# Token weights loaded by SP's queue and cast on chip, state totals as a piece of their own, and a new written order, in a fused RWKV-7 and WaveMLP kernel

## The chip, the core and the metric

The kernel runs on one core of a Trainium2 chip. A core has five engines with instruction streams of their own: TensorE (PE), VectorE (DVE), ScalarE (ACT), GpSimd (POOL) and SyncE (SP). DMA engines, 16 for the core, move data for whichever engine issues a transfer. The metric is device time in microseconds (us); lower is better.

## The reference

The first part is a recurrence over 768 tokens for 4 batches and 8 heads, with a 40 x 40 state per head. The second part mixes channels and tokens of the result.

```
for t in range(S):                       # B,H,S,D = 4,8,768,40
    y[:, :, t] = einsum('bhd,bhde->bhe', r_t, state)
    Sa = einsum('bhde,bhe->bhd', state, a_t)
    state = state * w_t[:, :, None, :] - einsum('bhd,bhe->bhde', Sa, b_t) \
          + einsum('bhd,bhe->bhde', v_t, k_t)
x = y.transpose(0, 2, 1, 3).reshape(B, S, H * D)      # 4 x 768 x 320
theta = x @ w_theta
zr, zi = x * cos(theta), x * sin(theta)
y2 = einsum('ts,bsd->btd', w_tok_r, zr) + einsum('ts,bsd->btd', w_tok_i, zi)
u = x + y2
out = u + maximum(u @ w_ch, 0)
```

The inputs and the output are float32.

## The kernel before

The tokens are cut into 24 chunks of 128 tokens (6 per batch); each chunk has its tokens on the 128 partitions and all 8 heads of 40 channels beside one another. Within a chunk the recurrence is turned into matrix products; from chunk to chunk of a batch only a small state (`gt`) goes on. Decay is made for two chunks at once: the logarithm of w (`LN`, ACT), sums of it along the tokens on PE (`CSI` inclusive, `CSE` exclusive, with the totals that the state needs), and their exponentials on ACT (`INVW`, `WI`). Then k and b are multiplied by the inverse decay (`KH`), a by the decay (`AH`), all are transposed on PE (`TRK`, `TRA`, `TRR`, `TRV`), and four score products of 128 x 128 per head are made (`PSI`, `PHI`, `LV`, `LU`), masked while they are taken out of PSUM (on DVE), or copied on ACT and masked on POOL (`MPSI` and the like). `X0`, `NU`, `GT` and `Y` use them. A chunk's result x goes through a transpose (`XT`), the product with w_theta (`TH`), cosine and sine on ACT (`SIN`), and a product with x (`ZR`). When a batch has its z, the token mixing follows (`YR`, 12 products for each of 6 blocks of rows), then u (`EU`), its transpose (`UT`), the channel product (`CH`), the output (`EO`) and its store (`ST`).

An entry of the order that starts with E is the eviction of a result from PSUM: `EXT` after `XT`, `EWT` after `WT`, `ENX` and `ENU` (negated copies) after `X0` and `NU`, and so on. A letter after an entry names its engine (A ACT, V DVE, G POOL). S stands for a DMA transpose through the crossbar, issued by SP in place of transposes on PE with an eviction. `@n` names a PSUM bank.

The order of the work is written out as the string `ORDER`. A loop at the end of the kernel runs through it and records each entry's instructions; every engine then runs its own in that order, so that an instruction that waits holds back all that stand behind it on its engine. `GI` adds the old state on PE, `EGA` does the same on DVE; a chunk has one or the other.

The token weights `w_tok_r` and `w_tok_i` (768 x 768, float32 in memory) come in rows of 128 x 768: `LDT:tb.n` is load number tb of weight n. Before, POOL issues it as a DMA that casts to bfloat16, into one of three buffers for each weight (`row_load`, line 723). `WT` transposes the row by six PE transposes, `EWT` copies it into place. Nearly all other loads are issued by SP, in the order's sequence; of the first ones, four (`LDK:0A`, `LDA:0A`, `LDB:1A`, `LDV:0A`) are issued by ACT. The landing buffers of k, b, a and v hold five chunks each, those of r and w three pairs. A load into a buffer in use waits on the issuing engine for its last reader.

Score products and decay sums use 64 of the array's 128 rows at a time, in two halves; all other matmuls use 128.

Of the kernel before, what the change touches and what calls it, by code (L numbers as in the profile page):

```python
# [19 lines left out]
LDW:0 LDK:0A LDB:0 LDA:0A LDA:1 LDB:1A LDK:1 LDV:0A LN:0A LDC:0.0G LDT:0.0G CSI:0@0 LDC:0.1G CSE:0@1 WI:0A  # L20
INVW:0A KH:0V TRK:0@0 AH:0V EKBT:0A TRA:0@3 LDW:2 EAT:0V LDR:0 KH:1V PHI:0@1 PSI:0@0
EPSI:0A MPSI:0G CV:0A LDB:2 EPHI:0A AH:1V TRK:1@1 EKBT:1V LN:2A TRA:1@2 MPHI:0G LDV:1 TRV:0@3
LDK:2 X0:0@0 EAT:1V CSI:2@0 CR:0A ENX:0V LDA:2 PSI:1@1 INVW:2A EVT:0V NU:0 ENU:0A EPSI:1V
TRR:0@1 PHI:1@0 LDB:3 ERT:0A GT:0@2 CV:1A LDK:3 CSE:2@1 EPHI:1V TRV:1@3 ERT:1A NUT:0@0 KH:2G
WI:2A EGT:0V LV:0@0 LDA:3 EVT:1V X0:1@1 ENX:1A ENUT:0A ELV:0V LDV:2 AH:2G GD:0@2 LDR:2 TRK:2@3
KH:3G LV:1@1 NU:1 EKBT:2A LU:0@0 ELV:1V LDW:4 TRA:2@0 ENU:1A LDV:3 ELU:0A NUT:1@3 AH:3G EAT:2V
GT:1@1 ENUT:1V PSI:2@1 TRK:3@0 EGD:0V EPSI:2V LDK:4 LDA:4 GI:1 EKBT:3A CV:2G TRA:3@3 LU:1@0
ELU:1A CR:2G PHI:2@1 EGT:1V X0:2@2 EAT:3V EPHI:2V MLU:0G ENX:2A LN:4A LDB:4 TRR:2@0 PSI:3@0
LDR:4 CV:3G PHI:3@1 MLU:1G Y:0@1 EPSI:3A MPSI:3G EPHI:3V NU:2 TRV:2@3 CSE:4@0 LDV:4 ENU:2A
ERT:2A EVT:2V GT:2@2 EX:0V WI:4A AH:4G CSI:4@1 INVW:4A Y:1@3 LDW:6 NUT:2@1 EGA:2V EGT:2V ERT:3A  # L30
ENUT:2V LV:2@0 LDA:5 TRV:3@2 EX:1V X0:3@1 ELV:2A KH:4G EVT:3V LU:2@1 ENX:3V ELU:2V LV:3@0
TRA:4@0 ELV:3A LDK:5 NU:3 TRK:4@3 LDB:5 GD:1@2 EAT:4V ENU:3A MLV:2G XT:0@0 EKBT:4V CR:4A GT:3@1
GI:3 EGD:1V EGT:3V PSI:4@1 EPSI:4V CV:4G PHI:4@0 LN:6A TRR:4@3 EPHI:4A NUT:3@2 MLV:3G Y:2@1
ENUT:3V LDB:6 LDA:6 AH:5G LDK:6 CSI:6@1 X0:4@2 EX:2V EXT:0A ERT:4A INVW:6A TRV:4@0 ENX:4V
MPHI:4G LDV:5 KH:5G LU:3@0 ERT:5A XT:1@1 NU:4 ELU:3V EXT:1A CSE:6@1 LDV:6 LDT:1.1G ENU:4A
TRA:5@3 WI:6A NUT:4@1 EVT:4V ENUT:4A TRK:5@2 LDK:7 EAT:5V AH:6G XT:2@0 EKBT:5V LV:4@0 TH:0@3
ELV:4V KH:6G PSI:5@1 GD:2@1 LDR:6 SIN:0A TH:1@2 LU:4@0 CV:5G GT:4@3 GI:4 EXT:2A EPSI:5V CV:6G
ZR:0G LDW:8 TRA:6@0 PHI:5@1 LDB:7 ELU:4A LDA:7 EGD:2V EGT:4V TH:2@1 SIN:1A EAT:6V MLU:4G SIN:2A
TRK:6@3 X0:5@0 GD:3@2 EPHI:5V EKBT:6V ENX:5A LDB:8 Y:3@1 ZR:1G EGD:3V EX:3V PSI:6@0 EPSI:6V
TRV:5@3 TRV:6@2 Y:4@1 LN:8A LDK:8 NU:5 PHI:6@1 EVT:6V ENU:5V EVT:5A CR:6G X0:6@2 EPHI:6V  # L40
LDT:1.0G KH:7G TRR:6@0 ENX:6A CSI:8@0 INVW:8A LDA:8 LDV:7 EX:4V NUT:5@3 LV:5@1 ELV:5A LDB:9
ERT:6V AH:7G ENUT:5V TRK:7@1 CSE:8@0 ERT:7V KH:8G TRA:7@3 WI:8A LDV:8 LV:6@1 EAT:7V EKBT:7V
ELV:6A LU:5@0 LDA:9 GD:4@0 NU:6 ELU:5V AH:8G PSI:7@1 TRK:8@3 LDK:9 ENU:6A EGD:4A CV:7A MLV:5G
PHI:7@0 EKBT:8A ZR:2G GT:6@1 NUT:6@2 EPSI:7V EPHI:7A EGT:6V TRV:7@0 TRA:8@3 ENUT:6V LDW:10
X0:7@1 EVT:7V LU:6@1 ENX:7V LV:7@0 LDR:8 ELU:6V Y:5@2 EX:5V EAT:8A XT:3@0 MPHI:7G AH:9G NU:7
EXT:3V XT:4@3 ELV:7A PSI:8@1 EXT:4A GD:6@2 KH:9G EPSI:8A EGD:6V TRA:9@0 LDV:9 PHI:8@0 TH:3@3
# [90 lines left out]
def kernel(  # L137
# [124 lines left out]

    tiles = [T() for _ in range(N)]
    keep = tc.keep_in_program_order
    queue = {"": nc.sync, "A": nc.scalar}
    eng = {"A": nc.scalar, "V": nc.vector, "G": nc.gpsimd}

    def copy(e, out, in_):
# [383 lines left out]
    def ev_three(i, e, name, src, tag, held):  # L652
        if e == "S":
            crossbar(i, name, xp, tag, held)
            return
# [178 lines left out]
```

## Time and profile before

| | us |
|---|---|
| median of 3 runs (206.68 to 207.59) | 207.25 |
| the profiled execution | 206.92 |
| its span, from the first to the last instruction | 205.2 |
| PE busy | 190.1 |
| DVE busy | 170.6 |
| ACT busy | 154.3 |
| POOL busy | 147.1 |

The granted TensorE clock was 0.999 of full speed. In the profile's rows, `L278` and `L282` are the helpers that record every matmul and every transpose, `L270`, `L272` and `L275` those for copies and products, so groups are told apart by tiles: `sc` and `sm` are the PSUM tiles of scores and of the rest, `kb`, `ah`, `v`, `r` the scaled inputs, `kbT`, `aT`, `rvT` their transposes. A row of groups reads: line, engine, operation, output <- inputs, shapes, count, then busy us and mean ns of one, then the engine's idle time ahead of them and what ended it. A row of the stretches of time gives, for each engine, busy us and the number of instructions. A row of the timeline gives start, length, and what it is. `ACTq` and `SPq` are issues of DMAs by those engines. "DMA to landing" counts from the issue.

### The profile page before, as it was taken

What the parts mean: (1) busy time and instruction counts of PE and PEld (TensorE: products, weight loads), DVE (VectorE), ACT (ScalarE), POOL (GpSimd) and SP (SyncE); (2) the same over time, 40 slices, a digit from 0 to 9 for tenths busy, and PEclk for the clock granted to TensorE, in tenths of its full rate; (3) what the DMA queues carried; (4) which work ended last, traced back from release to release, by engine and by line L of the source; (5) the groups of instructions that cost most, each with busy time, mean ns of one, the idle gap of its engine ahead of it and who ended that gap; (6) DMA issues with size and microseconds to landing.
All of it is one profiled execution on the core that took longest, in us unless ns stands there. A gap on an engine that the chain in (4) does not pass through costs nothing.

```text
span 205.2 us, 7809 instructions
## 1 busy us (share of the span) xinstructions
PE 190.1 (93%) x3266; PEld 147.5 (72%) x3266; DVE 170.6 (83%) x334; ACT 154.3 (75%) x259; POOL 147.1 (72%) x157
## 2 busy tenths in 40 slices
PE   0389999999999999999999999999999999999992
PEld 0166777877777887887887877887877787777671
DVE  7256899999999997999799998989888797975653
ACT  2367799997989997999899788987898685822100
POOL 8225778899989699998966886993989785634000
PEclk9999999999999999999999999999999999999999
DMA  7999999998898999899489989987979996433342
GB/s 136 187 240 159 225 171 178 173 230 140 153 221 154 213 159 216 164 213 226 103 171 193 192 172 238 192 135 161 169 97 154 218 129 140 99 90 103 102 150 96
DMA packets 144802, 34.17 MB, mean 167 GB/s; under 512 B 139520, under 2 KB 144768, under 8 KB 144768
## 3 DMA queue, kind: packets, MB, share of 16 engines
q1 hardware_dynamic: 138176, 30.26, 76.5%
q0 software_dynamic: 2432, 2.77, 8.4%
q10 hardware_dynamic: 4160, 0.66, 2.2%
q8 instruction: 25, 0.41, 0.9%
q14 instruction: 9, 0.07, 0.1%
HBM read 29.13 MB, written 3.93 MB: 161 GB/s over the span
## 4 chain that ended last, share of the span: by engine, by line
PE 80%; ACT 6%; DVE 5%; issue 2%; ACTq 2%; POOL 2%; POOLq 0%; DVEq 0%
PE sm L278 39%; PE sc L278 22%; PE sm L282 20%; ACTq L331 1%; ACT kbT L270 1%; ACT psi L270 1%; DVE phi L275 1%; ACTq L326 1%; ACT Wi_two L412 1%; ACT lw_two L338 1%; POOL z L275 1%; DVE lamu L275 1%; DVE rvT L272 1%; POOL lamv L554 1%; POOL phi L554 1%
## 5 line engine op out<-in xcount | busy, mean ns | idle before, releaser
L275 POOL TENSOR_TENSOR kb<-raw_kb,invW_two 128x640 bf16<-128x640 f32 x22 | 33.9, 1542 | 5.5 <-ACT invW_two L373 3.6
L275 POOL TENSOR_TENSOR z<-cs,x 128x640 bf16<-128x640 f32 x22 | 30.8, 1403 | 5.3 <-ACT cs L677 5.3
L278 PE MATMUL sm<-z,wtok_r 128*128 128x320 bf16 x120 | 34.3, 299 | 0.0
L278 PE MATMUL sm<-z,wtok_i 128*128 128x320 bf16 x120 | 34.2, 299 | 0.0
L275 POOL TENSOR_TENSOR ah<-raw_a,Wi_two 128x320 bf16<-128x320 f32 x22 | 19.0, 866 | 8.5 <-issue 5.2
L275 DVE TENSOR_TENSOR psi<-sc,mask_p 128x1024 bf16<-128x1024 f32 x16 | 19.5, 1219 | 1.0 <-PE sc L278 0.9
L554 POOL TENSOR_SCALAR_AFFINE_SELECT psi<-psi 128x1024 bf16<-128x1024 bf16 x8 | 8.7, 1093 | 14.0 <-ACT psi L270 11.6
L275 DVE TENSOR_TENSOR phi<-sc,mask_p 128x1024 bf16<-128x1024 f32 x14 | 17.1, 1219 | 1.6 <-PE sc L278 1.4
L278 PE MATMUL sc<-aT,kbT 64*128 64x128 bf16 x384 | 17.3, 225 | 1.1 <-ACT kbT L270 0.7
L275 DVE TENSOR_TENSOR lamu<-sc,mask_p 128x1024 bf16<-128x1024 f32 x14 | 17.1, 1220 | 0.6 <-PE sc L278 0.3
L282 PE MATMUL sm<-ident,kb 128*128 128x128 bf16 x184 | 14.9, 227 | 2.6 <-DVE kb L275 2.3
L278 PEld LDWEIGHTS <-wtok_r 128*128 128x128 bf16 x144 | 14.0, 97 | 4.6 <-issue 0.3
L270 ACT COPY rvT<-sm 128x512 bf16<-128x512 bf16 x28 | 15.9, 593 | 1.3 <-PE sm L282 0.7
L278 PEld LDWEIGHTS <-wtok_i 128*128 128x128 bf16 x144 | 14.1, 98 | 3.9 <-issue 0.2
L275 DVE TENSOR_TENSOR lamv<-sc,mask_p 128x1024 bf16<-128x1024 f32 x13 | 15.9, 1220 | 1.0 <-PE sc L278 0.5
L677 ACT ACTIVATE cs<-sm 128x320 f32<-128x320 f32 x26 | 9.9, 452 | 8.5 <-PE sm L278 8.4
L278 PEld LDWEIGHTS <-kbT 64*128 64x128 bf16 x384 | 11.9, 97 | 5.8 <-issue 2.4
L278 PEld LDWEIGHTS <-rvT 64*128 64x128 bf16 (+1 forms) x272 | 13.6, 95 | 2.9 <-issue 0.5
L278 PE MATMUL sm<-kb,lamv 128*128 128x40 bf16 x192 | 15.0, 180 | 0.0
L278 PE MATMUL sm<-kb,lamu 128*128 128x40 bf16 x192 | 14.9, 179 | 0.0
L282 PEld LDWEIGHTS <-kb 128*128 128x128 bf16 x184 | 11.5, 101 | 4.2 <-DVE kb L275 2.3
L554 POOL TENSOR_SCALAR_AFFINE_SELECT lamu<-lamu 128x1024 bf16<-128x1024 bf16 x10 | 10.9, 1090 | 4.1 <-ACT lamu L270 4.1
(137 smaller groups left out, 625.0 us busy)
## 6 DMA issues: line engine op xcount, KB each, us to landing
raw_w_two<-in_w_dram SPq DMA_DIRECT2D x12, 320.0 KB, 4.8
raw_r_two<-in_r_dram SPq DMA_DIRECT2D x12, 320.0 KB, 4.8
out_dram<-oo SPq DMA_DIRECT2D x24, 160.0 KB, 2.5
raw_kb<-in_b_dram SPq DMA_DIRECT2D x23, 160.0 KB, 4.6
raw_a<-in_a_dram SPq DMA_DIRECT2D x23, 160.0 KB, 4.5
raw_kb<-in_k_dram SPq DMA_DIRECT2D x23, 160.0 KB, 4.3
raw_v<-in_v_dram SPq DMA_DIRECT2D x23, 160.0 KB, 4.7
wtok_row<-in_moe_w_tok_r_dram POOLq DMA_DIRECT2D x6, 192.0 KB, 4.8
```

The source lines that it names most:

```text
L270: keep(nc.scalar.copy(out=out, in_=in_))
L272: keep(eng[e].tensor_copy(out=out, in_=in_))
L275: keep(eng[e].tensor_tensor(out=out, in0=in0, in1=in1, op=ALU.mult))
L278: keep(nc.tensor.matmul(out, lhsT=lhsT, rhs=rhs, start=start, stop=stop, skip_group_check=True))
L282: keep(nc.tensor.transpose(out=out, in_=in_, identity=ident))
L326: keep(queue[e].dma_start(out=tiles[i].raw_kb[:, j], in_=source(ap, i)))
L331: keep(queue[e].dma_start(out=t, in_=source(ap, i)))
L338: keep(nc.scalar.activation(out=q.lw[:, :, :, 0:D], in_=q.raw_w.rearrange("p h (j d) -> p j h d", j=2), func=AF.Ln))
L412: keep(nc.scalar.activation(out=two, in_=q.cse[:, LO:LO + 2 * DM + 16], func=AF.Exp))
L554: keep(nc.gpsimd.affine_select(out=flat, in_=flat, compare_op=ALU.is_ge, fill=0.0, base=-1, pattern=[[0, 2 * G], [1, 128]], channel_multip ...
L677: keep(nc.scalar.activation(out=cs[i % 5][:, c], in_=tiles[i].theta, func=AF.Sin, bias=(math.pi / 2, 0.0)[c]))
```

## The change

Three things are changed, and the order is written anew.

The rows of the token weights are loaded by SP as float32 into one landing buffer for each weight (`wraw`), and cast by a new entry `CW` on ACT (5 times) or POOL (7 times) into one bfloat16 buffer for each weight (`wrow`, three before). `WT` then works as before.

The totals of the decay over a chunk, nine small matmuls, are taken out of `CSE` and become the entry `CST`, which may stand anywhere between `CSE` and `WI`.

No load is issued by ACT any more. There are three theta buffers in place of four. The functions also get a way to handle two chunks' last 64 channels in one product (`THR`, `CHR`, `twin_x`, `twin_u`, `mix_ends`); the order holds no such entry, so the sets are empty and `XT`, `TH`, `UT` and `CH` do what they did.

In the new order the kinds of entries change as follows: `GI` from 5 to 8 and `EGA` from 11 to 8; `UT` from 14 to 19 and `XT` from 19 to 17, `GD` from 15 to 16, `NUT` from 20 to 21, `TRV` from 22 to 23, and so crossbar transfers from 28 to 22; PE runs 3290 matmuls and transposes in place of 3266. `ENX` and `ENU` on ACT go from 24 to 37, on DVE from 24 to 11; `ERT` and `EVT` on ACT from 28 to 19, on DVE from 18 to 28; masked evictions of scores on DVE from 57 to 59, on ACT from 39 to 37. ACT's table loads go from 14 to 12. The first row of the token weights is loaded behind the loads of chunk 9, not at the start.

```diff
@@ ORDER: the start, and the last rows of the token weights
-LDW:0 LDK:0A LDB:0 LDA:0A LDA:1 LDB:1A LDK:1 LDV:0A LN:0A LDC:0.0G LDT:0.0G CSI:0@0 LDC:0.1G CSE:0@1 WI:0A
-INVW:0A KH:0V TRK:0@0 AH:0V EKBT:0A TRA:0@3 LDW:2 EAT:0V LDR:0 KH:1V PHI:0@1 PSI:0@0
...
+LDC:0.2G LDW:2 LDW:0 LDB:0 LDK:0 LDC:0.0G LDA:0 LN:2A CSE:2@0 LDK:1 LDB:1 LN:0A CST:2 CSI:0@1
+WI:2A INVW:0A CSE:0@0 CST:0 WI:0A KH:0V LDV:0 LDA:1 TRK:0@0 AH:0V TRA:0@3 CSI:2@1 EAT:0V KH:1V
...
-    wrow = ctx.enter_context(tc.tile_pool(name="wrow", bufs=3))
+    wraw = ctx.enter_context(tc.tile_pool(name="wraw", bufs=1))
+    wrow = ctx.enter_context(tc.tile_pool(name="wrow", bufs=1))
...
-    th = mw.tile([128, 4, DM], FP32, name="th")
+    th = mw.tile([128, 3, DM], FP32, name="th")
...
@@ def cse(i, b):
             pair_sums(q.cse, q.lw, pair_exc)
-            tot = q.cse[:, LO + 2 * DM:LO + 2 * DM + 16]
-            mm(tot, ident, off_two.rearrange("p a g c -> p (a g c)"), True, False)
-            for g in range(G):
-                for j in range(2):
-                    mm(tot.rearrange("p (a n) -> p a n", a=2)[:, :, 2 * g:2 * g + 2],
-                       q.lw[:, j, 2 * g:2 * g + 2, :].rearrange("p a b -> p (a b)"),
-                       halves, False, j == 1)
             return
...
+    def totals(i):
+        q = tiles[i]
+        tot = q.cse[:, LO + 2 * DM:LO + 2 * DM + 16]
+        mm(tot, ident, off_two.rearrange("p a g c -> p (a g c)"), True, False)
+        for g in range(G):
+            for j in range(2):
+                mm(tot.rearrange("p (a n) -> p a n", a=2)[:, :, 2 * g:2 * g + 2],
+                   q.lw[:, j, 2 * g:2 * g + 2, :].rearrange("p a b -> p (a b)"),
+                   halves, False, j == 1)
...
     def row_load(tb, n):
-        wrows[tb, n] = tile_of(wrow, [128, S], BF16, f"wtok_row_{n}")
-        keep(nc.gpsimd.dma_start(out=wrows[tb, n],
-                                 in_=moe_w_tok[n][tb * 128:(tb + 1) * 128, :]))
+        wrows[tb, n] = tile_of(wraw, [128, S], FP32, f"wtok_raw_{n}")
+        keep(nc.sync.dma_start(out=wrows[tb, n], in_=moe_w_tok[n][tb * 128:(tb + 1) * 128, :]))
+
+    def row_cast(tb, n, e):
+        t = tile_of(wrow, [128, S], BF16, f"wtok_row_{n}")
+        copy(e, t, wrows[tb, n])
+        wrows[tb, n] = t
...
+        "CSE": lambda i, j, e, b: cse(i, b), "CST": lambda i, j, e, b: totals(i),
+        "LDT": lambda i, j, e, b: row_load(i, j), "CW": lambda i, j, e, b: row_cast(i, j, e),
```

How the instructions stand on three engines is shown next, each before and after. In the names a number is that of a buffer. First ACT, from its start: `raw_w_two` is the loaded w of a pair of chunks, `lw_two` its logarithm, `Wi_two` and `invW_two` the decay and its inverse. Before:

```order
L798 ACT_TABLE_LOAD
L326 DMA raw_kb<-in_k_dram 128x8x40
L331 DMA raw_a<-in_a_dram 128x8x40
L326 DMA raw_kb<-in_b_dram 128x8x40
L331 DMA raw_v<-in_v_dram 128x8x40
L338 ACTIVATE lw_two_93<-raw_w_two 128x16x40
L412 ACTIVATE Wi_two<-sc_237 128x656
L373 ACTIVATE invW_two<-sc_231 128x640
```

And ACT's start after (`lw_two_94` is the pair of chunks 2 and 3):

```order
L846 ACT_TABLE_LOAD
L357 ACTIVATE lw_two_94<-raw_w_two 128x16x40
L357 ACTIVATE lw_two_93<-raw_w_two 128x16x40
L434 ACTIVATE Wi_two<-sc_222 128x656
L392 ACTIVATE invW_two<-sc_240 128x640
L434 ACTIVATE Wi_two<-sc_249 128x656
L289 COPY kbT<-sm_270 128x1024
```

The four loads are gone from ACT, and the logarithm and decay of the second pair stand ahead of the inverse decay and the decay of the first.

Second PE, at the decay sums of chunks 20 and 21 (`pair_exc` is the triangle of ones that makes the sums, `off_two` and `halves` belong to the totals). Before:

```order
L278 LDWEIGHTS pair_exc
L278 MATMUL sc_3883<-lw_two_93,pair_exc 128x320
L278 LDWEIGHTS ident
L278 MATMUL sc_3883<-off_two,ident 128x16
L278 LDWEIGHTS lw_two_93
L278 MATMUL sc_3883<-halves,lw_two_93 128x2x2
```

And PE there after (`rvT` holds r and v transposed, so this is a score product, `LV` of chunk 18):

```order
L297 LDWEIGHTS pair_exc
L297 MATMUL sc_3884<-lw_two_93,pair_exc 128x320
L297 LDWEIGHTS rvT
L297 MATMUL sc_3889<-rvT 128x128
L297 LDWEIGHTS rvT
```

The totals, which use all 128 rows, no longer follow the sums; a score product, which uses 64 like the sums, does.

Third SP, in the stretch in which the loads of chunks 10 to 12 stand. Before (`x2` is two such loads in a row):

```order
L331 DMA raw_a<-in_a_dram 128x8x40
L326 DMA raw_kb<-in_k_dram 128x8x40
L326 DMA raw_kb<-in_b_dram 128x8x40 x2
L326 DMA raw_kb<-in_k_dram 128x8x40
L320 DMA raw_w_two<-in_w_dram 128x8x80
L331 DMA raw_v<-in_v_dram 128x8x40
```

And SP there after:

```order
L760 DMA wtok_raw_1676<-in_moe_w_tok_r_dram 128x768
L345 DMA raw_kb<-in_k_dram 128x8x40
L325 DMA raw_r_two<-in_r_dram 128x8x80
L760 DMA wtok_raw_1755<-in_moe_w_tok_i_dram 128x768
L350 DMA raw_v<-in_v_dram 128x8x40
L345 DMA raw_kb<-in_k_dram 128x8x40
L345 DMA raw_kb<-in_b_dram 128x8x40
L760 DMA wtok_raw_1892<-in_moe_w_tok_r_dram 128x768
L760 DMA wtok_raw_1922<-in_moe_w_tok_i_dram 128x768
L339 DMA raw_w_two<-in_w_dram 128x8x80
```

Four row loads of the token weights now stand among the chunk loads; each of these four goes into the buffer of an earlier row and waits for that row's cast, and the loads behind it wait with it.

333 lines of the change are left out of this document (184 added, 149 removed).

## Prediction

> **What bounds the kernel now.** I read the page's busy times, then its row of slices and the chain that ended last, then the busy time of four stretches.
>
> ```profile
> PE 190.1 (93%) x3266; PEld 147.5 (72%) x3266; DVE 170.6 (83%) x334; ACT 154.3 (75%) x259; POOL 147.1 (72%) x157
> PE   0389999999999999999999999999999999999992
> PE 80%; ACT 6%; DVE 5%; issue 2%; ACTq 2%; POOL 2%; POOLq 0%; DVEq 0%
> ```
>
> The last chain of work lies on PE for 80% of the span, and PE's slices are full from the fourth on. The stretches (PE, PE's weight loads, DVE, ACT, POOL; then clock, DMA share, GB/s) tell where it isn't full:
>
> ```profile
> 0.00:20.00 20.00, 10.29 (x117) 7.59 (x117) 10.87 (x56) 10.36 (x15) 9.24 (x20) 1.00 1.13 184
> 20.00:70.00 50.00, 48.50 (x995) 37.90 (x992) 47.28 (x79) 45.14 (x77) 42.94 (x45) 1.00 0.98 182
> 70.00:200.00 130.00, 129.74 (x2153) 101.39 (x2149) 110.48 (x197) 98.47 (x170) 94.92 (x93) 1.00 0.83 161
> 200.00:205.20 5.20, 1.58 (x11) 0.59 (x9) 1.92 (x5) 0.38 (x1) 0.00 (x0) 0.98 0.27 95
> ```
>
> There are three regimes. Up to 20 us PE idles for 9.7 us, and the DMA engines are full (share 1.13). From 20 to 70 us PE, DVE (47.28 of 50) and ACT are close together. From 70 to 200 us PE is busy for 129.74 of 130 us, so there a new order can win only by giving PE less to do. How PE's time is made up shows one row by row (start, length, instruction):
>
> ```profile
> 126.44 0.30 PE L278 MATMUL sm<-z,wtok_i 128*128 128x320 bf16 x1
> 126.57 0.33 PE L282 MATMUL sm<-ident,x 128*128 128x128 bf16 x3
> 126.74 0.30 PE L278 MATMUL sm<-z,wtok_r 128*128 128x320 bf16 x1
> 126.88 0.30 PE L278 MATMUL sm<-z,wtok_i 128*128 128x320 bf16 x1
> 127.11 0.62 PE L278 MATMUL sc<-aT,kbT 64*128 64x128 bf16 x16
> 127.66 0.31 PE L278 MATMUL sm<-z,wtok_r 128*128 128x320 bf16 x1
> ```
>
> Read the starts. A 320-column matmul takes 0.135 us until the next one starts (126.44 to 126.57), three 128-column transposes 0.17 (0.055 each). But ahead of the score matmuls, which use 64 rows of the array (64*128), the same 320-column matmul takes 0.23 (126.88 to 127.11). The step from 128 rows to 64 costs 0.095 us more, with nothing waited for. I take the same for the step back, which the row of 16 merges.
>
> **The change part by part.** The profiled execution took 206.92 us, with a span of 205.2; the median of the runs shown is 207.25, 0.33 above it.
>
> *PE's own work.* In the lists of matmuls the 64-row blocks (scores and decay sums, 120 in both) stand next to one another at 36 places before, at 53 after; splitting off the state totals lets a decay sum join a score block. Each joint saves a step in and a step out: 17 x 2 x 0.095 = 3.2 us. Against it stand 24 more matmuls (fewer transposes go by the crossbar, and three more old states are added on PE): 21 x 0.055 + 3 x 0.135 = 1.6 us. Net -1.6, on the path wherever PE is the limit. Ends: nothing, if all of it falls where DVE holds PE, and -3.2 if the added matmuls fill idle time. I take -1.6, since 130 us of the span are of the third regime.
>
> *The head.* ACT's rows, the landing of the first w load (counted from its issue), the first product on DVE, and two pieces of the chain:
>
> ```profile
> 0.83 0.49 ACTq L326 DMA_DIRECT2D raw_kb<-in_k_dram  x1
> 2.09 1.54 ACTq L326 DMA_DIRECT2D raw_kb<-in_b_dram  x1
> 3.65 1.71 ACTq L331 DMA_DIRECT2D raw_v<-in_v_dram  x1
> 5.41 0.74 ACT L338 ACTIVATE lw_two<-raw_w_two 128x640 bf16<-128x640 f32 x1 [3.33 <-DMA raw_w_two<-in_w_dram]
> 7.83 0.72 ACT L412 ACTIVATE Wi_two<-sc 128x656 f32<-128x656 f32 x1 [1.68 <-PE sc L278]
> 8.44 0.70 ACT L373 ACTIVATE invW_two<-sc 128x640 f32<-128x640 f32 x1
> ...
> DMA to landing us min/median/max: 4.0/4.0/4.0
> ...
> 9.17 0.83 DVE L275 TENSOR_TENSOR kb<-raw_kb,invW_two 128x640 bf16<-128x640 f32 x1 [3.76 <-ACT invW_two L373]
> ...
> 15.56 0.64 ACT lw_two L338
> 16.24 1.15 PE sc L278 x12
> ```
>
> w landed at 0.81 + 4.0 = 4.8 us, but ACT was issuing loads until 3.65 + 1.71 = 5.36, and the first logarithm starts at 5.41. Afterwards ACT issues nothing, two w loads go first, and three things change. (a) ACT is free when w lands; but w of chunk 0 is now second on SP, so it lands between 4.8 us and, with 320 KB more ahead of it at 184 GB/s, 1.8 later at 6.6. (b) The inverse decay comes ahead of the decay of its own pair, which took 0.72. From the start of the logarithm to the first kb product passed 9.17 - 5.41 = 3.76 us; 3.04 are left of it, so that the product starts between 7.9 and 9.6, a move of -1.3 to +0.5. (c) The second logarithm and its sums, on the chain at 15.56 and 16.24 (1.8 us), are done early, and the first row of the token weights, 1.2 us of all DMA engines, leaves the stretch where those are full. I take -1.5: the middle of that move, -0.4, and -1.1 of the 3.0 in (c), since the loads that follow still share full DMA engines. Ends: +0.5, and -3 (-1.3 and over half of (c)).
>
> A rule weighed there: the Trainium skill, "DMA: Bandwidth & Descriptors", section "Issuing engines are not separate DMA queues", says that DMAs of all issuing engines run on the same 16 DMA engines and a second issuer saves sequencer time only. By that rule taking four loads from ACT's queue delays no landing and the head gains up to 3; by the row, where ACT's first issue overlaps SP's, it could lose 0.5. The share of 1.13 with both queues at work agrees with the rule.
>
> *Row loads and casts.*
>
> ```profile
> L723 POOL DMA_DIRECT2D wtok_row<-in_moe_w_tok_r_dram x6 | 3.5, 580 | 0.0
> L272 POOL CAST r<-raw_r_two 128x640 bf16<-128x640 f32 x7 | 5.0, 720 | 0.0
> L270 ACT CAST r<-raw_r_two 128x640 bf16<-128x640 f32 x5 | 3.6, 729 | 0.0
> L677 ACT ACT_TABLE_LOAD x7 | 9.0, 1283 | 0.1
> L521 ACT ACTIVATE nx<-sm 128x320 bf16<-128x320 f32 x11 | 4.9, 442 | 2.1 <-PE sm L278 2.1
> L270 ACT COPY rvT<-sm 128x512 bf16<-128x512 bf16 x28 | 15.9, 593 | 1.3 <-PE sm L282 0.7 <-DVE rvT L272 0.5
> L523 DVE TENSOR_SCALAR nx<-sm 128x320 bf16<-128x320 f32 x13 | 6.4, 489 | 2.3 <-PE sm L278 2.0
> L272 DVE COPY rvT<-sm 128x512 bf16<-128x512 bf16 x18 | 8.8, 491 | 0.8 <-PE sm L282 0.7
> L275 DVE TENSOR_TENSOR psi<-sc,mask_p 128x1024 bf16<-128x1024 f32 x16 | 19.5, 1219 | 1.0 <-PE sc L278 0.9
> ...
> DMA to landing us min/median/max: 4.0/4.8/6.3
> ...
> raw_w_two<-in_w_dram SPq DMA_DIRECT2D x12, 320.0 KB, 4.8
> ```
>
> POOL loses twelve issues (12 x 0.58 = 7.0 us) and gains seven casts of 768 columns, 0.72 x 768/640 = 0.86 each, 6.0: nothing either way, with POOL busy 72%. ACT gains five casts, 5 x 0.87 = 4.4, and 13 negated copies at 0.44 (5.7), and loses nine copies of r and v at 0.59 (5.3) and two table loads at 1.28 (2.6); with its smaller moves about +2. DVE gets ten such copies (4.9) and two masked products (2.4) and loses 13 negated copies (6.4): about +0.5. ACT's +2 spreads over 185 us in which it is busy three quarters, so PE's work covers it; uncovered, it would cost 2.
>
> What has a price is SP's queue, which takes over 16 loads (twelve rows, four from ACT) and loses six of 28 crossbar transfers; the bytes are the same, so the DMA engines' work is too. A row's landing buffer is single, so from its third row load on SP stops until the cast of an earlier row is done, and the loads of k, b, a, v, r, w wait behind it. The places are close: behind the sixth row load stands w of pair 12, whose logarithm comes 129 matmuls after the cast that is waited for; 130 us / 2153 = 0.060 us per matmul makes that 7.8 us. From it go the cast (0.87), the row load's share of all DMA engines (1.2) and the landing (4.8): 0.9 us is left. Between the two casts of rows 3 and 4 on POOL stand 107 matmuls, 6.4 us, against a cast and a landing of 5.7. A landing at the slow end (6.3) turns both into waits of about 0.7. Bounds: 0, and +6 (ten such loads at 0.6). I take +1.0, near the lower end, because 4.8 is the usual landing.
>
> *Everything else that the new order moves* (where evictions stand, three theta buffers in place of four, the end): +0.2. The nearest row is PE's 0.26 us of idle time in 130 us, which a new order can hardly better and can easily miss: between 0 and +3, taken near the lower end, as the last 5 us stand almost as they did.
>
> Sum: -1.6 - 1.5 + 1.0 + 0.2 = -1.9, so 205.0 for the profiled execution and 205.3 for the median.
>
> **The rivals.** *DVE holds the middle.* With 47.28 of 50 us busy from 20 to 70 us and 0.5 more to do, DVE gives back the head's lead and the joints there: -1.6 x 130/200 = -1.0 stays, +1.0 for the loads: 206.9, median 207.2, no change. For it: the DVE row. Against it: its work starts earlier too.
>
> *The loads come late (slower).* Place: SP's queue behind the row loads. Point: a row landing over 5.6 us after its issue. Eight of the ten stops then cost PE the 0.7 worked out above, 5.6 in place of 1.0: 209.6, median 209.9. For it: the largest landing, 6.3, and a DMA share of 0.98. Against it: loads have little to answer for in the list of waits (total, times, longest):
>
> ```profile
> POOL psi L554 <- DMA raw_kb<-in_k_dram: 2.5, 1, 2.5
> POOL kb L275 <- DMA raw_kb<-in_b_dram: 1.7, 1, 1.7
> ```
>
> *The casts cost ACT.* ACT's five casts stand ahead of evictions for which PE waits: 4.4 us are uncovered, 205.0 + 4.4 = 209.4, median 209.7. Against it: ACT's 75%. In the Trainium skill, "DMA: Bandwidth & Descriptors", section "Rules for kernel authors" has a cast during DMA issued from GpSimd, which is what the change gives up; no run so far shows which is cheaper here.
>
> *The late crossbar transfers were no loss.* PE's list of waits names none of them, so counting them brings nothing by itself; no term of the sum rests on it.
>
> **How the numbers follow.** Forecast 0.52; DVE holds 0.17; late loads 0.18; casts 0.05; a new wait elsewhere in the order 0.08, slower. Half a per cent, about what a measurement of this kernel can tell from no change, is 1.0 us: 206.2 to 208.3. Faster takes the forecast and a little of the second (0.56), the same most of the second (0.17), slower the rest (0.27). The range goes from 202.7 (head -3, loads 0, joints -1.6, order 0, plus 0.33) to 209.0, into the late loads with seven stops of 0.7 in place of eight; the forecast alone would lie between 203.5 and 206.5.
>
> **What would show it.** Right: score rows that follow one another without the 0.23 step, and PE busy near 188 us; the first kb product before 9 us; PE idle under 9 us up to 20 us. Wrong: waits of kb, v or a wtok cast for DMA between 50 and 105 us, or PE below 48 of 50 us from 20 to 70 us, and SP's own waits on casts of several us.

## The result: no change that can be measured

| | us |
|---|---|
| forecast | 205.3 (202.7 to 209.0) |
| after, median of 20 runs | 208.04 (206.36 to 209.49) |
| before, median of 20 runs beside it | 207.66 (206.62 to 210.12) |
| ratio after / before | 1.0007, 95% interval 0.9988 to 1.0025 |
| profiled execution after | 209.23, span 207.5 |

The forecast was a gain of 1%; the interval leaves at most a gain of 0.12%. The profiled execution after lies 1.2 us above its median, that of before 0.7 below the median in this table, so the two profiles side by side overstate the loss by 1.9. Medians are of all runs of a kernel, ratios leave out the runs that took over 1.5% longer than its fastest, so a ratio need not be the quotient of two medians.

The page after: busy times, PE's slices, and the chain that ended last, by engine.

```profile
PE 189.3 (91%) x3290; PEld 147.1 (71%) x3290; DVE 171.7 (83%) x332; ACT 157.7 (76%) x269; POOL 144.2 (69%) x148
PE   0886999999699989999899999999999999999992
PE 59%; DMA 13%; POOL 7%; DVE 6%; SPq 6%; ACT 4%; issue 3%; POOLq 0%; ACTq 0%; DVEq 0%
```

PE's share of the chain fell from 80% to 59%, and DMA, which was not in it, holds 13%. PE's slices are full earlier than before, and then have gaps. The stretches (PE, weight loads, DVE, ACT, POOL; clock, DMA share, GB/s):

```profile
0.00:20.00 20.00, 11.91 (x179) 8.29 (x180) 12.49 (x58) 14.16 (x21) 9.94 (x21) 1.00 1.03 177
20.00:70.00 50.00, 46.10 (x984) 37.56 (x982) 47.56 (x75) 45.81 (x80) 41.64 (x43) 1.00 0.97 198
70.00:200.00 130.00, 127.44 (x2106) 98.97 (x2103) 107.97 (x194) 96.79 (x169) 92.58 (x86) 1.00 0.79 167
```

By 20 us PE is 1.6 us ahead of before; from 20 to 70 us it is busy for 2.4 us less, and from 70 to 200 for 2.3 less. What holds it shows in five rows of the list of waits of all engines (total, times, longest) and in five pieces of the chain (start, length):

```profile
POOL kb L294 <- DMA raw_kb<-in_b_dram: 4.7, 5, 1.8
PE sm L301 <- POOL kb L294: 3.6, 3, 1.3
ACT lw_two L357 <- DMA raw_w_two<-in_w_dram: 3.4, 4, 2.0
ACT v L289 <- DMA raw_v<-in_v_dram: 2.9, 4, 1.7
POOL v L291 <- DMA raw_v<-in_v_dram: 2.8, 2, 2.6
...
11.18 4.72 DMA raw_kb<-in_b_dram
...
28.14 5.34 DMA raw_w_two<-in_w_dram
...
46.32 5.09 DMA raw_kb<-in_b_dram
...
66.54 5.80 DMA raw_kb<-in_b_dram
...
95.23 5.65 DMA raw_v<-in_v_dram
```

Loads of b, w and v now end waits on POOL and ACT, and PE waits for POOL's product kb behind them. In the trace before, the loads of chunks 4 to 8 land 1.6 to 7.7 us ahead of their use. After, some load of each of the chunks 4, 5, 6 and 8 lands 0.0 to 0.2 us ahead, and of chunk 7 0.5. They land no sooner than before: k and b of chunk 8 at 49.2 and 51.4 us, before at 49.5 and 48.9.

The two mechanisms of the forecast are both there. The head (ACT, then DVE, then the start of a score block in PE's list at 155 us):

```profile
4.12 0.74 ACT L357 ACTIVATE lw_two<-raw_w_two 128x640 bf16<-128x640 f32 x1 [2.04 <-DMA raw_w_two<-in_w_dram]
...
7.66 0.82 DVE L294 TENSOR_TENSOR kb<-raw_kb,invW_two 128x640 bf16<-128x640 f32 x1 [2.24 <-ACT invW_two L392]
...
155.13 0.45 PE L297 MATMUL sc<-lw_two,pair_exc 64*128 64x320 bf16 x4
155.41 0.39 PE L297 MATMUL sc<-rvT 64*128 64x128 bf16 x8
```

The first logarithm starts at 4.12 in place of 5.41, the first kb product at 7.66 in place of 9.17. And the score block follows the four decay sums 0.28 us after their start, two pairs at the 0.135 that a 320-column matmul takes: the 0.095 of a step is gone there. The price itself holds all over the trace before: ahead of a 64-row block a 320-column matmul takes 0.232 us in place of 0.136 (median of 23 places), a 128-column one 0.152 in place of 0.056 (36 places). The step back, which the forecast took to be the same, costs it too: behind the last 128-column matmul of a block it is 0.148 until the next 128-row matmul starts, in place of 0.053 to the next pair within a block (63 places).

To set waits apart from work I gave each matmul of a list the interval to the next start that its size and its neighbour take where nothing is waited for (the intervals of the forecast), and counted the rest as waiting. A shorter list is thus fewer and cheaper matmuls at those prices. The tail runs from the last start to the end of the span. All in us; one profile each, and kernels with the order of before differ by 2 us in the last column, so only larger differences are read from it.

| kernel | first matmul | PE's list without waits | waits to 20 us | 20 to 70 | 70 to the last start | tail | span |
|---|---|---|---|---|---|---|---|
| before | 6.2 | 179.0 | 8.5 | 4.8 | 2.9 | 3.8 | 205.2 |
| after | 4.9 | 177.3 | 7.0 | 6.9 | 7.6 | 3.9 | 207.5 |
| late_head | 7.9 | 177.3 | 5.6 | 5.9 | 6.0 | 3.9 | 206.6 |
| flat_after | 5.0 | 177.3 | 6.6 | 5.0 | 5.1 | 3.9 | 202.9 |

From before to after the list is 1.7 shorter and the head 2.8 earlier (1.3 at the first matmul, 1.5 in waits up to 20 us). 6.8 us of new waits behind 20 us take that back, in this slower one of its executions.

### The profile page after: what moved, and what is told of

It reads as the page before. It is cut to its first block, busy times and chain, and to the rows that moved or that the text cites. A ratio compares the mean times of both kernels' runs of the same rounds, so it can differ in the third digit from the quotient of the medians.

```text
span 207.5 us, 7860 instructions
## 1 busy us (share of the span) xinstructions
PE 189.3 (91%) x3290; PEld 147.1 (71%) x3290; DVE 171.7 (83%) x332; ACT 157.7 (76%) x269; POOL 144.2 (69%) x148
## 4 chain that ended last, share of the span: by engine, by line
PE 59%; DMA 13%; POOL 7%; DVE 6%; SPq 6%; ACT 4%; issue 3%; POOLq 0%; ACTq 0%; DVEq 0%
PE sm L297 33%; PE sc L297 13%; PE sm L301 12%; DMA raw_kb<-in_b_dram 8%; POOL kb L294 3%; DMA raw_v<-in_v_dram 3%; DMA raw_w_two<-in_w_dram 3%; SPq L345 3%; SPq L350 2%; DVE rvT L291 2%; DVE lamv L294 2%; ACT psi L289 1%; SPq L325 1%; POOL wtok_row L291 1%; POOL z L294 1%
## 5 line engine op out<-in xcount | busy, mean ns | idle before, releaser
L294 POOL TENSOR_TENSOR z<-cs,x_two 128x640 bf16<-128x640 f32 x22 | 30.9, 1407 | 4.0 <-ACT cs L715 3.9
L294 DVE TENSOR_TENSOR phi<-sc,mask_p 128x1024 bf16<-128x1024 f32 x15 | 18.3, 1218 | 2.6 <-PE sc L297 2.5
L294 DVE TENSOR_TENSOR lamv<-sc,mask_p 128x1024 bf16<-128x1024 f32 x16 | 19.5, 1216 | 1.1 <-PE sc L297 1.0
L294 DVE TENSOR_TENSOR lamu<-sc,mask_p 128x1024 bf16<-128x1024 f32 x15 | 18.3, 1217 | 2.1 <-PE sc L297 2.0
L576 POOL TENSOR_SCALAR_AFFINE_SELECT psi<-psi 128x1024 bf16<-128x1024 bf16 x11 | 12.0, 1092 | 7.3 <-ACT psi L289 7.3
L294 DVE TENSOR_TENSOR psi<-sc,mask_p 128x1024 bf16<-128x1024 f32 x13 | 15.8, 1217 | 1.3 <-PE sc L297 1.2
L291 DVE COPY rvT<-sm 128x512 bf16<-128x512 bf16 x28 | 14.6, 539 | 1.4 <-PE sm L301 1.1
L576 POOL TENSOR_SCALAR_AFFINE_SELECT phi<-phi 128x1024 bf16<-128x1024 bf16 x9 | 9.9, 1095 | 8.1 <-ACT phi L289 8.1
L752 DVE SCALAR_TENSOR_TENSOR oo<-sm,u 128x320 f32<-128x320 f32 x24 | 11.5, 488 | 4.2 <-PE sm L297 4.0
L297 PE MATMUL sm<-kb,lamu 128*128 128x40 bf16 x192 | 14.9, 179 | 0.0
```

The source lines that it names most:

```text
L291: keep(eng[e].tensor_copy(out=out, in_=in_))
L294: keep(eng[e].tensor_tensor(out=out, in0=in0, in1=in1, op=ALU.mult))
L297: keep(nc.tensor.matmul(out, lhsT=lhsT, rhs=rhs, start=start, stop=stop, skip_group_check=True))
L576: keep(nc.gpsimd.affine_select(out=flat, in_=flat, compare_op=ALU.is_ge, fill=0.0, base=-1, pattern=[[0, 2 * G], [1, 128]], channel_multip ...
L752: keep(nc.vector.scalar_tensor_tensor(out=q.oo, in0=q.ops[:, 0:DM], scalar=0.0, in1=q.u, op0=ALU.max, op1=ALU.add))
```

## The experiments

Theory 1: the loads of k, b, a, v, w, r can't land sooner than they do, since the DMA engines are full, so that the lead of the head and of the joints is given back as waiting for them. Theory 2: row loads on SP and their casts cost what the rest gains. Theory 3: DVE holds PE. Ratios are to the kernel before, run beside each on the same chip, with 95% intervals; 0.5% is 1.0 us.

### Is it the loads?

The reads of k, b, a and v of chunks 2 and later are made of runs of 1280 bytes in place of 160 (a token's 40 floats). As many bytes are loaded, but of tokens and heads in another order, so the output is of other data. The edit, in the changed kernel (flat_after) and in the kernel before (flat_before):

```diff
-        return ap[bi, :, ci * C:(ci + 1) * C, :].rearrange("h t d -> t h d")
+        if i < 2:
+            return ap[bi, :, ci * C:(ci + 1) * C, :].rearrange("h t d -> t h d")
+        rows_of = ap[bi].rearrange("h t d -> (h t d)").rearrange("(n p f) -> n p f", n=NCH, p=C)
+        return rows_of[ci].rearrange("p (h d) -> p h d", h=H)
```

> The changed kernel, with k, b, a and v of chunks 2 to 23 read from memory in runs of 1280 bytes instead of 160, so that each of these loads keeps the DMA engines busy for about half as long; the tokens come in another order, so the output is another, and nothing else changes. Theory 1 (chunk loads cannot land sooner, because the 16 DMA engines are full up to 110 us, and so PE's lead is given back): PE's waits for loads between 20 and 110 us go, 203.5 to 204.5 us. Theory 2 (the row loads stop SP's queue until a cast is done): about half of it goes, 206 us. Theory 3 (DVE holds the middle): 208 us, unchanged.

> The same edit in the kernel before. Theory 1: that kernel hardly waits for loads after 20 us, so it gains only in the head and where loads come late: 205.5 to 207 us, 2 to 3 us above the changed kernel with the edit. Theory 3: 207.5, and no difference between the two with the edit.

flat_after 204.62 us, 0.984 (0.979 to 0.989). flat_before 209.33 us, 1.002 (0.997 to 1.006). The same relief of the DMA engines is worth 1.6% to the changed kernel and nothing to the one before. So with early loads the changed kernel gains 1.6% where 1% was forecast. For flat_before theory 1 missed: it expected 205.5 to 207 us. By the count above PE waits 1.5 us less up to 20 us in its profile, but behind that for two DMAs for which it doesn't wait in the profile before, a row of token weights and a crossbar transpose:

```profile
PE sm L282 <- DMA wtok_row<-in_moe_w_tok_i_dram: 1.1, 1, 1.1
PE sm L278 <- DMA uT<-u: 0.9, 1, 0.9
```

The stretches of after and, below the dots, of flat_after, with SP's longest waits for a cast:

```profile
20.00:30.00 10.00, 9.29 (x211) 7.70 (x209) 9.65 (x15) 8.90 (x15) 8.68 (x9) 1.00 1.00 194
50.00:60.00 10.00, 8.21 (x168) 6.42 (x166) 8.95 (x16) 9.13 (x16) 6.77 (x8) 1.00 0.92 211
...
20.00:30.00 10.00, 9.54 (x215) 7.97 (x214) 9.51 (x16) 8.70 (x15) 8.42 (x10) 1.00 1.06 306
50.00:60.00 10.00, 9.54 (x196) 7.54 (x195) 9.97 (x17) 9.71 (x20) 8.78 (x10) 1.00 0.26 74
...
SPq L763 <- POOL wtok_row L291: 23.7, 3, 11.6
```

At a DMA share of 1.00 loads in runs of 160 bytes move 194 GB/s, in runs of 1280 bytes 306 (share 1.06); w and r come in runs of 320 bytes in both. With the long runs SP has issued all loads up to the third row load by 44 us and stands there until 56.4, 11.6 us of it waiting for the cast of an earlier row; the share falls to 0.26, and PE is busy for 9.54 in place of 8.21. So the stop behind row loads that the forecast priced exists here, and the loads behind it, of chunks 10 and 11, still land 0.7 us or more ahead of their use. The Trainium skill, "DMA: Bandwidth & Descriptors", section "Why small descriptors are slow (HBM only)", tells of a fixed cost for each packet and each descriptor; these rows agree with its direction.

DVE is busier in flat_after (9.97 of 10) while PE does more, so theory 3 falls: it does not hold PE at the level of the changed kernel.

Where the loads matter was tried with long runs for chunks 2 to 9 alone (flat_early):

```diff
-        if i < 2:
+        if i < 2 or i > 9:
```

> Runs of 1280 bytes for k, b, a and v of chunks 2 to 9 only; all later chunks are read as the changed kernel does (tokens of chunks 2 to 9 in another order, so the output is of other data). Theory 1 (the loads of the first 50 us are the bound, since only there are the DMA engines full without any margin): most of the 3.4 us that all flat chunks gained, so 204.6 to 206. Rival (the loss is at the loads from 60 to 110 us, among the row loads): at most 1 us of gain, 207 to 208.

205.99 us, 0.989 (0.984 to 0.994): 1.1 of the 1.6% lies at the loads of the first 50 us, as theory 1 has it. The other 0.5% would be at later loads, but the two intervals overlap.

### Is the head's lead worth anything?

The first logarithm is run five times over, which delays PE's start by 2.9 us: in the changed kernel (late_head), in flat_after (flat_late) and in the kernel before (before_late, with `i == 0`).

```diff
-            keep(nc.scalar.activation(
-                out=q.lw[:, :, :, 0:D], in_=q.raw_w.rearrange("p h (j d) -> p j h d", j=2),
-                func=AF.Ln))
+            for _ in range(5 if i == 2 else 1):
+                keep(nc.scalar.activation(
+                    out=q.lw[:, :, :, 0:D], in_=q.raw_w.rearrange("p h (j d) -> p j h d", j=2),
+                    func=AF.Ln))
```

> The changed kernel with the first logarithm run five times over in place of once, the same values each time: four more of 0.74 us stand ahead of the first decay sums, so that PE starts 2.9 us later (first matmul at 7.8 us in place of 4.9, first kb product at 10.6 in place of 7.7). That takes away the whole lead that the head has over the kernel before. Theory 1 (the loads of chunks 2 to 9 can't land sooner, and PE waits for them, so the lead is given back anyway): the waits of kb, v and the logarithms for loads between 10 and 60 us shrink by what is lost at the start; 208.0 + 0 to 0.8 us. Rival (PE's own work sets the end, the waits for loads are beside it): 208.0 + 2.9 = 210.9.

> The same four extra logarithms in the kernel whose k, b, a and v loads from chunk 2 on are read in runs of 1280 bytes (tokens in another order, so the output is of other data). There the loads land 4 to 17 us ahead of use from 20 us on. Theory 1: nothing is left that the lead could be given back to, so the delay stays: 204.6 + 2.9 = 207.5, at least 206.8. Rival (the start is not on the path, whatever the loads do): 204.6 + 0 to 0.5.

> The kernel before with its first logarithm run five times over in place of once: 4 x 0.74 = 2.9 us more ahead of the first products. There the loads of chunks 4 to 9 land 2 to 7 us ahead of their use. Theory 1 (a lead or a lag at the start is kept where the loads have a margin, and given back where they have none): 207.7 + 2.9 = 210.6, at least 209.8. Rival (the loads pace the first 50 us in this kernel too, so its start is free): 207.7 + 0 to 0.8.

| kernel | us | ratio | against the same kernel without the delay |
|---|---|---|---|
| late_head | 208.16 | 0.999 (0.995 to 1.003) | -0.2% |
| flat_late | 207.56 | 0.997 (0.994 to 1.000) | +1.3% |
| before_late | 210.98 | 1.012 (1.008 to 1.016) | +1.2% |

1.2% is 2.6 us, 1.3% is 2.7. Where loads have a margin, a lag of 2.9 at the start is a lag of 2.6 or 2.7 at the end; in the changed kernel it costs nothing (-0.2%, give or take 0.4). The timelines show the place, the kb product of chunk 8. One row each of before, after, late_head, flat_after and flat_late:

```profile
51.79 1.53 POOL L275 TENSOR_TENSOR kb<-raw_kb,invW_two 128x640 bf16<-128x640 f32 x1
...
51.57 1.54 POOL L294 TENSOR_TENSOR kb<-raw_kb,invW_two 128x640 bf16<-128x640 f32 x1 [1.37 <-DMA raw_kb<-in_b_dram]
...
51.86 1.55 POOL L294 TENSOR_TENSOR kb<-raw_kb,invW_two 128x640 bf16<-128x640 f32 x1 [0.23 <-ACT invW_two L393]
...
49.36 1.54 POOL L294 TENSOR_TENSOR kb<-raw_kb,invW_two 128x640 bf16<-128x640 f32 x1 [0.21 <-ACT invW_two L395]
...
51.86 1.54 POOL L294 TENSOR_TENSOR kb<-raw_kb,invW_two 128x640 bf16<-128x640 f32 x1 [0.22 <-ACT invW_two L396]
```

The changed kernel starts its first product 1.5 us before the old one and this product 0.2 us before it; the wait of 1.37 for b is what remains of the lead. late_head starts 2.75 us later than after and is there 0.3 later, without the wait. Only flat_after keeps the lead.

The pace can be worked out. A chunk needs four loads of 160 KB and half of two of 320 KB, 960 KB or 983,000 bytes. At 194 GB/s that is 5.1 us, at the 182 of the old kernel's stretch from 20 to 70 us 5.4. From its first to its ninth kb product the changed kernel takes (51.57 - 7.66) / 8 = 5.5 us for a chunk: it can't be ahead of its loads. Nor do the landing buffers hold the loads back: in the trace after, each load of k, b, a, v, w and r of chunks 5 to 9 is issued 14.9 us or more after the last reader of its buffer is done.

### SP's queue or the DMA engines behind it?

SP issues loads back to back from 19 to 51 us in the changed kernel: 27 in 29.8 us. In split_pool the v loads of chunks 2 to 9 are issued by POOL, at the same places of the order (a G behind the eight entries).

```diff
-LDV:2
+LDV:2G
...
-    def load(ap, name, i):
+    def load(ap, name, i, e=nc.sync):
...
-        keep(nc.sync.dma_start(out=t, in_=source(ap, i)))
+        keep(e.dma_start(out=t, in_=source(ap, i)))
```

> The changed kernel with the v loads of chunks 2 to 9 issued by POOL, at the same places of the written order, and no longer by SP. SP issues loads back to back from 19 to 51 us, 0.5 to 2.1 us each, so either SP's issuing is what makes the loads late or the DMA engines behind it are full. Theory 1 (the DMA engines are full): SP's issues get shorter or start earlier, the loads still land as late, 208.0 within 0.8. Rival (SP's queue is the limit): eight issues of about 1.1 us leave it, the b load of chunk 8 lands 4 us or more ahead of its use in place of 0.2, and the time goes to between 205 and 206.5.

211.01 us, 1.010 (1.004 to 1.017): slower, which neither side expected. From 18.8 to 47.4 us SP issues 22 loads and POOL five more: 27 in 28.6 us, hardly more than SP alone in the changed kernel (0.94 for each us against 0.91), and SP's own issues are now 1.3 us apart in place of 1.1. The stretch, and a wait that grew:

```profile
20.00:70.00 50.00, 43.44 (x900) 34.72 (x901) 43.64 (x71) 42.19 (x73) 45.21 (x47) 1.00 0.94 190
...
POOL v L291 <- DMA raw_v<-in_v_dram: 6.2, 4, 2.8
```

190 GB/s in place of 198. A second issuer brings hardly more loads and SP's own issues take longer, so the limit is behind the queue. The rival's sign did come: b of chunk 8 lands 7.8 us ahead of its use, at 48.2 us in place of 51.4, with the use 4.4 us later. But v, which stands on POOL behind POOL's work, comes late (of chunk 7 at 54.3 in place of 48.1 us), so POOL waits 6.2 us for v in place of 2.8. The Trainium skill, "DMA: Bandwidth & Descriptors", section "Issuing engines are not separate DMA queues", says that a second issuer saves only the sequencer's time; the trace agrees, with 190 GB/s for two issuers and 198 for one.

The four early loads were also given back to ACT in the changed kernel (act_loads):

```diff
-LDC:0.2G LDW:2 LDW:0 LDB:0 LDK:0 LDC:0.0G LDA:0 LN:2A CSE:2@0 LDK:1 LDB:1 LN:0A CST:2 CSI:0@1
+LDC:0.2G LDW:2 LDK:0A LDW:0 LDA:0A LDB:0 LDB:1A LDC:0.0G LDV:0A LN:2A CSE:2@0 LDK:1 LN:0A CST:2 CSI:0@1
```

> The changed kernel with four early loads (k and a and v of chunk 0, b of chunk 1) issued by ACT again, near where the kernel before has them; all the rest as changed. ACT issues until about 5 us, so the first logarithm and the first matmul come up to 1 us later than 4.1 and 4.9. Theory 1 (the head's lead is given back at the loads): 208.0 within 0.7, with shorter waits for loads after it. Rival (the forecast's reading, ACT's issuing holds the head): 208.0 + 0.5 to 1.3. A gain of up to 1 us would say that a second issuer brings the first loads earlier, which neither has.

208.77 us, 1.002 (0.998 to 1.006). The first kb product and that of chunk 8:

```profile
9.07 0.83 DVE L294 TENSOR_TENSOR kb<-raw_kb,invW_two 128x640 bf16<-128x640 f32 x1 [3.66 <-ACT invW_two L392]
...
51.61 1.53 POOL L294 TENSOR_TENSOR kb<-raw_kb,invW_two 128x640 bf16<-128x640 f32 x1 [1.27 <-DMA raw_kb<-in_b_dram]
```

The start is 1.4 us later, as the forecast's reading of ACT has it, and at chunk 8 nothing of that is left. That reading was right; at the end it is worth nothing that the interval shows (0.2% against the change).

Last, the chunk loads were put in the order in which flat_after uses them, where buffers allow it (after_edf; 39 entries change places, nine of them up to the loads of chunk 9, as in `LDA:3 ... LDV:2 LDR:2` to `LDR:2 ... LDA:3 LDV:2`).

> The changed kernel with its chunk loads put in the order in which they are used when no load is late (39 of 120 loads change places on SP's queue, nearly all behind 55 us, nothing else changes). Theory 1 (up to 50 us the DMA engines are full and the order is already that of use): at most the waits for loads between 65 and 110 us go, 1.5 us in the profile, so 206.5 to 208.0. Rival (a better order of loads would have saved the lead): 204.5 to 206.

209.84 us, 1.005 (1.001 to 1.008): slightly slower, which neither side expected. This order, the only other one tried, doesn't save the lead.

### Row loads and casts

rows_pool takes the row part out of the changed kernel: POOL loads the rows as casting DMAs into three buffers, and `CW` does nothing. rows_tiny keeps the loads on SP and the casts, but fetches 40 of 768 columns of the token weights, so the product with them is not the reference's. The first edit below is that of rows_pool, the second that of rows_tiny.

```diff
-        wrows[tb, n] = tile_of(wraw, [128, S], FP32, f"wtok_raw_{n}")
-        keep(nc.sync.dma_start(out=wrows[tb, n], in_=moe_w_tok[n][tb * 128:(tb + 1) * 128, :]))
+        wrows[tb, n] = tile_of(wrow, [128, S], BF16, f"wtok_row_{n}")
+        keep(nc.gpsimd.dma_start(out=wrows[tb, n], in_=moe_w_tok[n][tb * 128:(tb + 1) * 128, :]))
...
-        wrows[tb, n] = tile_of(wraw, [128, S], FP32, f"wtok_raw_{n}")
-        keep(nc.sync.dma_start(out=wrows[tb, n], in_=moe_w_tok[n][tb * 128:(tb + 1) * 128, :]))
+        wrows[tb, n] = raw_row[n]
+        keep(nc.sync.dma_start(out=raw_row[n][:, 0:40],
+                               in_=moe_w_tok[n][tb * 128:(tb + 1) * 128, 0:40]))
```

> The changed kernel with the rows loaded as before the change: POOL issues a casting DMA into three buffers, at the same entries of the order, and the casts on ACT and POOL fall away. SP's queue has no row loads. Theory 1: the DMA engines have the same work, 207 to 208 us. Theory 2: nothing stops SP for a cast, 204.5 to 205.5 us. Theory 3: 207.5 to 208 us, as DVE has the same work.

> The changed kernel, whose row loads fetch 40 of 768 columns (the rest of the landing buffer is zero, so the output is another); the places, buffers, waits and casts of the rows stay. It takes away the bytes of the rows, 15 us of all DMA engines, and leaves the stops of SP's queue at casts. Theory 1: 204.5 to 205.5 us. Theory 2: 207 us or more, since the stops stay. Theory 3: 208 us.

rows_pool 208.08 us, 1.000 (0.996 to 1.003); rows_tiny 208.69 us, 1.000 (0.997 to 1.004). Neither taking the loads off SP and dropping the casts, nor taking away nearly all the rows' bytes, is worth anything that the intervals show (0.4%, 0.8 us). Theory 2 falls for the changed kernel. In the profile of rows_tiny PE is busier where the rows stood; the stretch in after, then in rows_tiny:

```profile
70.00:110.00 40.00, 37.95 (x695) 30.44 (x693) 36.50 (x66) 33.36 (x56) 33.33 (x32) 1.00 0.96 212
...
70.00:110.00 40.00, 39.63 (x711) 31.69 (x706) 37.99 (x68) 34.74 (x59) 34.80 (x33) 1.00 0.84 152
```

PE is busy for 1.7 us more there in one profile, and the medians don't show it.

before_rows does the row part alone in the kernel before: loads by SP, casts `CW`, three theta buffers, two bfloat16 buffers for each weight, the entries put between those of the old order.

```diff
-        wrows[tb, n] = tile_of(wrow, [128, S], BF16, f"wtok_row_{n}")
-        keep(nc.gpsimd.dma_start(out=wrows[tb, n],
-                                 in_=moe_w_tok[n][tb * 128:(tb + 1) * 128, :]))
+        wrows[tb, n] = tile_of(wraw, [128, S], FP32, f"wtok_raw_{n}")
+        keep(nc.sync.dma_start(out=wrows[tb, n], in_=moe_w_tok[n][tb * 128:(tb + 1) * 128, :]))
...
+    def row_cast(tb, n, e):
+        t = tile_of(wrow, [128, S], BF16, f"wtok_row_{n}")
+        copy(e, t, wrows[tb, n])
+        wrows[tb, n] = t
```

> The kernel before with only the row part of the change: token weights loaded by SP as float32 into one landing buffer for each weight, cast on ACT (5) or POOL (7) into two bfloat16 buffers for each, three theta buffers; the order else as before, with the row loads and casts put between its entries. Theory 1 (row loads on SP and the casts cost nothing that can be measured): 207.7 within 0.8. Rival (the forecast's term, 1.0 and up to 6): 208.7 or more, with waits of k, b, a, v loads on SP behind row loads.

211.04 us, 1.012 (1.004 to 1.020): outside what theory 1 allows (0.8 us), with 2.5. SP's longest single wait ahead of a load is 2.0 us, and by the count of waits PE loses 1.1 more from 20 to 70 us and 2.8 more from 70 to 200, 1.0 of that for a crossbar transpose (`uT<-u`). I placed these entries by hand, with nothing else moved, so this doesn't tell the price of the row part from the price of my places; that stays open.

### Joints of 64-row blocks

totals_in writes the totals behind the decay sums again in the changed kernel, which takes four joints away.

```diff
             pair_sums(q.cse, q.lw, pair_exc)
+            totals(i)
...
-        "CSE": lambda i, j, e, b: cse(i, b), "CST": lambda i, j, e, b: totals(i),
+        "CSE": lambda i, j, e, b: cse(i, b), "CST": lambda i, j, e, b: None,
```

> The changed kernel with the nine totals matmuls written behind the decay sums again. That takes four joints of 64-row blocks away (71 blocks in place of 67, counting PE's list): 4 x 2 x 0.095 = 0.8 us more of PE's work, somewhat less in the time where PE waits for loads. So 208.0 + 0.4 to 0.8 by the forecast's price of a joint; the rival is that the step between 64 and 128 rows is hidden and costs nothing: 208.0 within 0.3. A median alone may not tell these apart; the profile's PE rows should.

210.09 us, 1.008 (1.003 to 1.013), against 1.001 for the change: about 1.5 us slower, for a price of 0.8. The sign is as forecast, and the interval (0.3 to 2.7 us) holds both, and not zero.

Then joints alone were made in the kernel before: the totals get an entry, and sums move by a few entries to stand beside a score block or another sum (some exponentials on ACT move with them). before_joints makes eleven more, joints_late only seven, those of chunks 10 to 22.

```diff
-PHI:13@1 EUT:0A
+PHI:13@1 CSE:14@0 EUT:0A
...
-CSI:20@0 TRK:19@0 EX:16V UT:6@1 CSE:20@1
+CSI:20@0 CSE:20@1 TRK:19@0 EX:16V UT:6@1 CST:20
```

> The kernel before with only the joints: the totals are an entry of their own, and seven decay sums of the order are moved by a few entries, and four totals behind the next score block, so that PE's list has 73 blocks of 64-row matmuls in place of 84. The loads, the row part, the head, the counts of matmuls and transposes stay. By the forecast's price, 11 x 2 x 0.095 = 2.1 us less of PE's work. Since the loads of this kernel have a margin of 2 to 7 us up to chunk 9, the gain should be kept: 207.7 - 2.1 = 205.6, at most 206.6. Rival (a step is hidden behind something else, or a moved sum makes a new wait on ACT): 207.7 within 0.5.

> The same with only those joints that lie behind 50 us, of chunks 10 to 22: 77 blocks in place of 84, 7 x 2 x 0.095 = 1.3 us less of PE's work. By the forecast's price 207.7 - 1.3 = 206.4. Rival: 207.7 within 0.5. If this gains as much as the kernel with all eleven, the joints in the first 50 us are worth nothing in this kernel either.

before_joints 211.44 us, 1.016 (1.011 to 1.021); joints_late 211.86 us, 1.015 (1.011 to 1.020): slower, which neither side allowed, though PE's list without waits is 176.9 and 177.6 in place of 179.0. PE's waits grew by more. One of the new ones, from PE's list of waits in before_joints from 90 to 150 us, and the chain there:

```profile
PE sc L253 <- DVE psi L250: 1.1, 1, 1.1
...
97.75 1.24 DVE psi L250
```

`CSE:14` now follows `PHI:13` at once, but its PSUM bank is that of `PSI:13`, whose eviction on DVE takes 1.24 us; PE waits for it where 0.19 was to be saved. joints_few leaves such moves out and keeps six.

> The kernel before with six joints more (78 blocks of 64-row matmuls in place of 84), only those where the moved sum finds its PSUM bank empty for some microseconds already, so that no wait of 0.3 us or more for DVE or ACT should stand ahead of it, as it did in the kernel with eleven. By the price of a joint 6 x 2 x 0.095 = 1.1 us less: 207.7 - 1.1 = 206.6, with PE's other waits as before. Rival (any move of a sum costs more in waits than the joint saves): 208 or more. If PE's matmul rows shrink by 1.1 and its waits grow by as much, the joint's price is right and it is the order around it that decides.

208.25 us, 0.997 (0.994 to 1.0005): -0.6 us, between -1.3 and +0.1, for a price of -1.1. So the price of a step is not refuted, and not shown to the full either; what a joint costs in waits for a bank can be several times what it saves. By its ratio it is the fastest kernel here that computes the reference, and the interval does not set it apart from the one before.

## Why the prediction was wrong, step by step

**PE's own work, -1.6: right as work.** The list without waits shrank by 1.7, the row at 155 us shows a joint, and the price of a step holds both ways in the median of its places. That the time falls by as much is not shown: taken alone in the kernel before, six joints measured about half their price, and not clear of nothing. PE's busy time, which I named as a sign, can't show this: the same 3290 matmuls read 189.0 in flat_after and 191.2 in flat_early.

**The head, -1.5: mechanism right, larger than forecast, and worth nothing.** 1.3 at the first matmul and 1.5 up to 20 us make -2.8; kb at 7.66 and 8.1 us of idle PE are inside the marks that I set. But the sum counted it as time saved at the end. late_head and act_loads start 2.9 and 1.4 us later, and the time stays.

**Row loads and casts, +1.0: this is the step that failed.** I priced late loads only as stops of SP behind row loads, and closed the rest with "the bytes are the same, so the DMA engines' work is too". The work is the same, but the time in which it was needed was not: I had moved its user ahead by 1.5 us and more. The price of that, 0.989 against 1.001 for chunks 2 to 9 and 0.984 for all, is 2.5 to 3.4 us (1.2% and 1.65%), and it begins at 16 us, while the first row load is issued at 52.9. The row loads and casts themselves measured nothing in the changed kernel. What the forecast could have read in the trace before: each of the chunks 4 to 8 has a load that lands only 1.6 to 2.8 us ahead of its use there, so a lead of 2.8 at 20 us uses that up. The share of 1.13 up to 20 us and 0.98 up to 70 stood quoted in the prediction; in the head I used it to cut one term from 3.0 to 1.1, and did not ask by when the ninth chunk can have landed.

**The order, +0.2: too small by an unknown part.** In flat_after, where loads are early, PE still waits 5.1 us behind 70 us against 2.9 before. Single waits there are below 0.5 us; but kernels with the old order show 2.9 to 5.0 in that column, so the excess is between nothing and 2.2. The upper figures there are in part single waits for DMAs that come in some executions, as the two of flat_before; how much of them a usual execution of the kernel before has, no run settles.

The sum with these sizes (the list and the head from one profile each, the loads from ratios): -1.7 for the list, -2.8 for the head, 2.5 to 3.4 for the loads, and 0 to 2.2 for the order lies between -2.0 and +1.1; measured is +0.15 (1.0007).

**The rivals.** The loads did come late, but at the chunk loads, not behind the row loads; eight stops of 0.7 did not occur, and what was lost equals what was gained, so that the time is the same and not slower. DVE in the middle gave the right number, 207.2, by luck: flat_after rules its mechanism out. (DVE's added work was also mis-summed, 4.9 + 2.4 - 6.4 is 0.9 and not 0.5; the pages show 1.1. No term of the sum rests on it.) The casts on ACT cost nothing that can be measured (rows_pool has none). That PE's waits name no crossbar transpose was so in the one profile that the forecast had: in flat_before, joints_few, joints_late and before_rows, all built on the old order, PE waits 0.7 to 1.0 us for `uT<-u`. Of the signs for "wrong", two came: waits of kb and v for DMA between 50 and 105 us, and PE at 46.10 of 50. The third hardly: ahead of row loads SP waits 3.0 us in all, at most 1.4.

## What to carry to other kernels

Before a lead is added to the sum, ask who else must be early: where the DMA engines' share is near 1, divide the bytes that one step needs by the GB/s of that stretch, and compare with the time that the step takes now; with the two equal, an earlier start is paid back at the next load. The test is cheap: delay the start, and if the time stays, the start was not on the path. And work taken from the bounding engine by moving an instruction counts only if what it waits for, here the reader of its PSUM bank, is done by then.

## What the runs showed that was not expected

Delaying PE's start by 2.9 us changed the time by -0.2% in one order and by +1.2% in the other, with the same loads and nearly the same matmuls. Eight loads of 160 KB moved from SP to POOL cost 1.0%; POOL's issues of 0.92 us each and the places that the loads then had both come into question, and no run tells them apart. And a shorter list of matmuls made a kernel slower by 1.6%, through new waits, the longest found 1.1 us.
